# Earlier constants for a state-space layer, and a last output tile cut in 448 and 128 columns

## Chip, cores and metric

The kernel runs on one core of one Trainium2 chip. The metric is the device time of one execution in microseconds; I quote medians of several executions. A profile's own span is 1.8 us shorter than the time of the same execution.

## The reference, cut to what matters

```python
xn = layernorm(x)                                # x: 2048 x 576, bf16
# A: a diagonal state-space layer with 576 complex states
dt      = exp(log_dt)
Lam_bar = exp(dt * (Lambda_re + 1j * Lambda_im))
B_bar   = ((Lam_bar - 1) / Lam)[:, None] * (B_re + 1j * B_im)
h_t     = Lam_bar * h_(t-1) + B_bar @ xn_t       # a recurrence over 2048 steps
y_t     = 2 * real(C @ h_t) + xn_t * Dskip
# B: a gated layer
out = x + y + (sigmoid(xn @ w_gate) * (xn @ w_up)) @ w_down    # 576 -> 4608 -> 576
```

Nearly all arithmetic is in B's three products. A needs three vectors of 576 numbers (`log_dt`, `Lambda_re`, `Lambda_im`), here "the constants", from which the kernel makes two Exps and ten tables of 512 sines or cosines.

## The kernel before

TensorE (PE) does one "group" after another: 128 rows of gate and up for a block of 512 tokens, 18 matmuls, 1.94 us. ScalarE (ACT) takes a group's two halves out of PSUM (sigmoid into `sT`, copy into `uT`), VectorE (DVE) multiplies them into `hT`. PSUM holds four such pairs in turn, so group n + 4 needs the pair of group n. The first slot of the program has 24 groups; then eight output tiles `pd` take the products `hT` in.

Smaller work is queued in a list with costs. After every group the list is given some credit and emits what it can pay for, so the place of an instruction on its engine is fixed when the kernel is built:

```python
class GateUp:
    def evac(self):
        ...
        nc.scalar.activation(sT[:], self.ps[:, 0, :], ACT.Sigmoid)
        nc.scalar.copy(uT[:], self.ps[:, 1, :])
        h = hpool.tile([P, TB], BF16, name="hT", bufs=2 * FC)
        nc.vector.tensor_mul(h[:], sT[:], uT[:])
        ...
        bg.step(...)                 # emits queued work behind this group

def exp_first():
    nc.scalar.activation(dt[:], ldt[:], ACT.Exp)
    nc.vector.tensor_mul(r5[:], dt[:], lre[:])
    nc.scalar.activation(r5[:], r5[:], ACT.Exp)

# ... the queue of the first slot, in this order
for tt in range(0, 2 * TT_B):
    bg.add(1.25, lambda tt=tt: ln_resid(tt))     # 8 residual sums on VectorE
bg.gap()
bg.add(1.0, exp_first, ready=lambda: consts_at[0] is not None and consts_at[0] + 4 <= bg.now)
bg.gap()
bg.add(1.5, angles_small)
for pt in range(NU):                             # NU = 5
    for which in range(2):
        bg.add(1.35, lambda pt=pt, which=which: angle(pt, which))   # 10 angle tables on VectorE
```

`load_consts` is called among the loads of the second half of the first slot. The last output tile is computed in two halves of 288 columns, so that the first half is added and stored beside the second half's matmuls.

Of the kernel before, what the change touches and what calls it, by code (L numbers as in the profile page):

```python
# [66 lines left out]
def kernel(  # L67
# [17 lines left out]
    nc = tc.nc  # L85
    P = 128
# [3 lines left out]
    S, D = x.shape  # L90
# [15 lines left out]
    DH = D // 2  # L106
# [21 lines left out]
    def ps_pair(name):  # L128
        return psum.tile([P, 2, TB], FP32, name=name, tag="ps")
# [57 lines left out]
    lre = consts.tile([P, NU], FP32, name="lre")  # L187
    lim = consts.tile([P, NU], FP32, name="lim")
    ldt = consts.tile([P, NU], FP32, name="ldt")
    consts_at = [None]  # L190

    def load_consts():
        for (dst, src) in ((ldt, A_log_dt), (lre, A_Lambda_re), (lim, A_Lambda_im)):
            nc.gpsimd.dma_start(dst[:, 0:PT], src[0:R0].rearrange("(a p) -> p a", p=P))
            for h0 in (0, H):
                nc.gpsimd.dma_start(dst[h0:h0 + H, PT:NU], src[R0:NS].rearrange("(a b) -> a b", b=1))
        consts_at[0] = bg.now

    iota = ssmp.tile([P, TB], FP32, name="iota", tag="buim", bufs=2)
    nc.gpsimd.iota(iota[:], pattern=[[1, TB]], base=0, channel_multiplier=0,  # L200
                   allow_small_or_imprecise_dtypes=True)
# [79 lines left out]
    def split_bt():  # L281
# [8 lines left out]
    bt_loads = [  # L290
        lambda: nc.sync.dma_start_transpose(ctre[:], A_B_re[:, 0:R0]),
        lambda: nc.sync.dma_start_transpose(ctp[:], A_B_re[:, WN:D]),
        lambda: nc.sync.dma_start_transpose(ctim[:], A_B_im[:, 0:R0]),
        lambda: nc.sync.dma_start_transpose(ctw[:], A_B_im[:, WN:D]),
    ]
# [184 lines left out]
    bg = Background()  # L480
# [69 lines left out]
    def halves(ap):  # L550
        return ap.rearrange("p (a b) -> p a b", a=2)
# [10 lines left out]
    def d_step(tt, terms, final, last=False):  # L562
        acc = accs[tt]
        n = len(terms)
        pd = None if last else ps_pair("pd")

        def mm(out, i, a):
            lhsT, rhs = terms[i]
            nc.tensor.matmul(out, lhsT, rhs[:, a * DH:(a + 1) * DH], start=i == 0, stop=i == n - 1)  # L569

        if last:
            ob = lnp.tile([P, D], BF16, name="ob", bufs=2)
            for a, eng in ((0, nc.sync), (1, nc.scalar)):
                cs = slice(a * DH, (a + 1) * DH)
                pd = ps_pair("pd")
                for i in range(n):
                    mm(pd[:, 0, 0:DH], i, a)
                nc.vector.tensor_add(ob[:, cs], acc[:, cs], pd[:, 0, 0:DH])
                eng.dma_start(o[tt * P:(tt + 1) * P, cs], ob[:, cs])
            return  # L580
        for i in range(n):
            for a in range(2):
                mm(pd[:, a, 0:DH], i, a)
        if final:
            ob = lnp.tile([P, D], BF16, name="ob", bufs=2)
            nc.vector.tensor_add(halves(ob[:]), halves(acc[:]), pd[:, :, 0:DH])  # L586
            nc.sync.dma_start(o[tt * P:(tt + 1) * P, :], ob[:])
        else:
            nc.vector.tensor_add(halves(acc[:]), halves(acc[:]), pd[:, :, 0:DH])  # L589
        bg.step(n * T_DTERM - 0.76 - 0.2)  # L590


    def queue_ln(nb, part):

        tts = list(range(nb * TT_B, (nb + 1) * TT_B))

        def add(cost, fn, ready=None):
            bg.add(cost, fn, ready, urgent=True)

        if part == 0:  # L600
            for tt in tts:
                add(0.0, lambda tt=tt: load_x(tt, nc.sync))
            bg.gap(True)
            bg.gap(True)
            for tt in tts:
                add(1.05, lambda tt=tt: ln_stats(tt))
            bg.gap(True)
            add(0.0, lambda: ln_std(nb, 0, TT_B))
            bg.gap(True)
            add(0.2, lambda: ln_recip(nb, 0, TT_B))  # L610
        if part == 1:
            for tt in tts:
                add(0.9, lambda tt=tt: ln_norm(tt))
                add(0.0, lambda tt=tt: ln_dma_transpose(tt))
            add(0.0, lambda: ln_done.add(nb))
        if part == 2:
            for tt in tts:
                add(1.25, lambda tt=tt: ln_resid(tt), ready=lambda tt=tt: acc_free[0] > tt - 2 * TT_B)
                if nb == 2:
                    add(0.9, lambda tt=tt: ln_norm(tt + TT_B))  # L620
                    add(0.0, lambda tt=tt: ln_dma_transpose(tt + TT_B))
            if nb == 2:
                add(0.0, lambda: ln_done.add(3))
# [9 lines left out]
    def want_bu(i):  # L633
        if i < len(chain):
            bu_wanted.append(chain[i])

    def queue_ssm(i):
        nb, pt = chain[i]

        def bu_ready():  # L640
            return (nb, pt) in bu and bu_at[(nb, pt)] + 2 <= bg.now

        def h_ready():
            return nb < 2 or (nb - 2) in c_done

        bg.add(1.85, lambda: ssm_w(nb, pt, 0), ready=bu_ready)
        if pt < PT:
            bg.add(1.85, lambda: ssm_w(nb, pt, 1))
        else:
            bg.add(0.0, lambda: None)  # L650
        bg.add(0.0, lambda: want_bu(i + 2))
        bg.add(1.3, lambda: ssm_scan(nb, pt, 0))
        bg.add(2.0 if pt < PT else 1.2, lambda: ssm_scan(nb, pt, 1))
        bg.add(1.3, lambda: ssm_h(nb, pt, 0), ready=h_ready)
        if pt < PT:
            bg.add(1.3, lambda: ssm_h(nb, pt, 1))
        if pt == NU - 1:
            bg.add(0.0, lambda: ssm_done.add(nb))
# [55 lines left out]
    side_loads = deque()  # L714
# [68 lines left out]
    for tt in range(0, 2 * TT_B):  # L783
        bg.add(1.25, lambda tt=tt: ln_resid(tt))
    bg.gap()
    bg.add(1.0, exp_first, ready=lambda: consts_at[0] is not None and consts_at[0] + 4 <= bg.now)
    bg.gap()
    bg.add(1.5, angles_small)
    for pt in range(NU):
# [12 lines left out]
    for sb in range(NSB):  # L802
        b0 = sb * NB_SB
        for c in range(NC):
            slot = sb * NC + c
            if slot == 0:
                order = [(f, 0) for f in range(2, 10)] + [(f, 1) for f in range(0, 10)]
                order += [(f, nb) for nb in range(2) for f in range(10, 12)]
            else:
                order = [(f, b0 + nbl) for fq in range(0, FC, 4) for nbl in range(NB_SB) for f in range(fq, fq + 4)]  # L810
            if slot == 1:
                side_loads.extend(ct_loads)
                bg.add(0.0, lambda: want_bu(0))
                bg.add(0.0, lambda: want_bu(1))
                for i in range(len(chain)):
                    queue_ssm(i)
            if slot == 2:
                queue_ln(2, 0)
                queue_ln(2, 1)
            if slot == 0:  # L820
                run_groups([GateUp(slot, f, nb) for (f, nb) in order[:8]])
                catch_up_ln(1)
                order = order[8:]
                side_loads.extend([load_consts] + bt_loads)
            run_groups([GateUp(slot, f, nb) for (f, nb) in order])
            if slot == 0:
                split_bt()
                bg.add(0.0, sines)
                bg.gap()
                bg.add(2.9, per_state_q)  # L830
                for pt in range(NU):
                    bg.add(1.2, lambda pt=pt: tables(pt, 0))
                    bg.add(2.1, lambda pt=pt: tables(pt, 1))
            if slot == 2:
                catch_up(0)
                catch_up_ln(2)
                queue_ln(3, 0)
                queue_ln(2, 2)
                queue_ln(3, 2)
            for tt in range(NB_SB * TT_B):  # L840
                nbl, tl = divmod(tt, TT_B)
                nb = b0 + nbl
                final = c == NC - 1 and (nb != 1 or 1 in ssm_done)
                if final:
                    catch_up(nb)
                terms = [(hT[(f, nb)][:, tl * P:(tl + 1) * P], wd_t[(slot, f // FP)][:, f % FP, :]) for f in range(FC)]
                if final:
                    terms += c_terms(nb, tl)
                d_step(sb * NB_SB * TT_B + tt, terms, final, last=slot == n_slots - 1 and tt == NB_SB * TT_B - 1)
                if slot == 2 and final:  # L850
                    acc_free[0] = tt + 1
                if slot == 2 and tt == TT_B - 1:
                    c_done.add(0)
                if slot == 2 and tt == NB_SB * TT_B - 1:
                    glu_done[0] = True
                    if final:
                        c_done.add(1)
                between_steps()
# [30 lines left out]
```

## Time and profile before

| | before |
|---|---|
| median of 3 runs (lowest, highest) | 508.96 us (508.66, 509.38) |
| span of the profiled run | 506.5 us |
| PE busy | 500.9 us, 99% |
| VectorE, ScalarE, GpSimd busy | 64%, 40%, 19% |
| granted TensorE clock | 1.00 |

A busy share of 99% for PE says that what the other engines do can matter only where it makes PE wait. Those waits have a list of their own: who waited for whom, total, times, longest. The prediction below shows it, and the timelines around the one wait in reach; a line of a timeline is start, duration, engine, line of the kernel, operation, output and inputs, and in brackets how long the engine had been idle and what ended that.

### The profile page before, as it was taken

The page shows a single profiled execution, that of the slowest core. Times are in us where ns is not written, and L with a number is a line of the kernel's source. Part 1 is how long each engine was busy: PE and PEld are TensorE (multiplying, and loading weights), DVE is VectorE, ACT ScalarE, POOL GpSimd, SP SyncE. Part 2 cuts the span into 40 slices and gives each one's busy share as a digit, 9 for nine tenths or more (in the row PEclk, how much of TensorE's full clock was granted, in tenths as well). Part 3 has the DMA queues.
Part 4 walks back from the last instruction along what each step waited for, and adds up shares of the span by engine and source line. Part 5 has one row for each costly group of instructions (what it writes and reads, how often), then busy time and mean ns, then how long its engine had stood idle before and what let it go on. Part 6 is the DMA issues. An engine that isn't in the chain of part 4 may idle for free.

```text
span 506.5 us, 10662 instructions
## 1 busy us (share of the span) xinstructions
PE 500.9 (99%) x4536; PEld 290.1 (57%) x4536; DVE 324.1 (64%) x703; ACT 204.9 (40%) x368; POOL 96.9 (19%) x143
## 2 busy tenths in 40 slices
PE   8999999999999999999999999999999999999997
PEld 6444575444477444477754444774444774446775
DVE  6964999886888797868878767786765222221111
ACT  4767623556500756520035655006555005553000
POOL 7138420123100043110001231000431001300000
PEclk9999999999999999999999999999999999999999
DMA  8999895246220099261430652200753201600001
GB/s 211 206 181 163 204 188 98 55 110 141 49 48 25 1 145 199 58 149 37 89 77 11 155 132 55 49 25 1 160 114 79 48 25 39 171 1 4 33 25 36
DMA packets 42959, 45.59 MB, mean 90 GB/s; under 512 B 30496, under 2 KB 34336, under 8 KB 42912
## 3 DMA queue, kind: packets, MB, share of 16 engines
q0 software_dynamic: 12672, 34.23, 31.1%
q1 hardware_dynamic: 29808, 10.33, 10.7%
q8 instruction: 35, 0.57, 0.5%
q10 hardware_dynamic: 432, 0.37, 0.2%
q14 instruction: 12, 0.10, 0.1%
HBM read 34.36 MB, written 2.36 MB: 72 GB/s over the span
## 4 chain that ended last, share of the span: by engine, by line
PE 94%; DVE 3%; ACT 1%; DMA 1%; issue 0%
PE pgu L495 52%; PE pd L569 34%; PE pbu L524 7%; DVE sctab L325 1%; DVE rnd L324 1%; DMA xt<-in_A_x_dram 1%; DVE ang L349 1%; PE ptr L741 0%; DVE hT L504 0%; ACT xT L744 0%; DVE bnst L224 0%; ACT L328 0%; ACT uT L502 0%; ACT L501 0%; ACT sT L501 0%
## 5 line engine op out<-in xcount | busy, mean ns | idle before, releaser
L495 PE MATMUL pgu<-xT,wgu 64*128 64x512 bf16 (+1 forms) x2628 | 283.7, 373 | 0.0
L495 PEld LDWEIGHTS <-wgu 64*128 64x128 bf16 x2628 | 127.6, 94 | 151.1 <-issue 0.5
L569 PE MATMUL pd<-wd,hT 128*128 128x288 bf16 x1152 | 144.8, 286 | 0.4 <-DVE hT L504 0.4
L501 ACT ACTIVATE sT<-pgu 128x512 bf16<-128x512 f32 x144 | 86.4, 600 | 120.4 <-PE pgu L495 110.3
L569 PEld LDWEIGHTS <-hT 128*128 128x128 bf16 x1152 | 112.1, 98 | 31.3 <-DVE hT L504 1.5
L504 DVE TENSOR_TENSOR hT<-sT,uT 128x512 bf16<-128x512 bf16 x144 | 60.7, 423 | 100.3 <-ACT uT L502 100.1
L502 ACT CAST uT<-pgu 128x512 bf16<-128x512 f32 x144 | 83.9, 583 | 0.0
L154 POOL DMA_DIRECT2D wgu<-in_B_w_gate_dram x36 | 27.9, 776 | 227.2 <-PE pgu L495 208.2
L160 POOL DMA_DIRECT2D wd<-in_B_w_down_dram x36 | 26.6, 755 | 100.2 <-PE pd L569 100.2
L530 ACT COPY bure<-pbu 128x512 f32<-128x512 f32 x16 | 9.4, 588 | 87.8 <-PE pbu L524 75.4
L589 DVE TENSOR_TENSOR acc<-acc,pd 128x576 f32<-128x576 f32 x32 | 24.1, 752 | 24.5 <-PE pd L569 24.5
L586 DVE TENSOR_TENSOR ob<-acc,pd 128x576 bf16<-128x576 f32 x15 | 11.3, 754 | 38.0 <-PE pd L569 38.0
L524 PE MATMUL pbu<-xT,bt 64*128 64x512 bf16 x288 | 33.7, 376 | 0.0
L569 PEld LDWEIGHTS <-hst 128*128 128x128 bf16 x288 | 28.2, 98 | 7.1
L154 POOL DMA_DIRECT2D wgu<-in_B_w_up_dram x36 | 26.8, 745 | 2.7 <-DMA wgu<-in_B_w_up_dram 1.9
L569 PE MATMUL pd<-ctre,hst 128*128 128x288 bf16 x128 | 26.5, 286 | 0.0
L569 PE MATMUL pd<-ctim,hst 128*128 128x288 bf16 x128 | 26.5, 286 | 0.0
L439 DVE TENSOR_TENSOR_SCAN gre<-r,g0re,wrim 128x512 bf16<-128x512 f32 x20 | 25.6, 1279 | 0.0
L524 PEld LDWEIGHTS <-bt 64*128 64x128 bf16 x288 | 13.7, 94 | 17.1 <-issue 0.7
L446 DVE TENSOR_TENSOR_SCAN gim<-r,g0im,wrim 128x512 bf16<-128x512 f32 x16 | 20.4, 1275 | 0.0
L224 DVE BATCH_NORM_STATS2 bnst<-xt 128x6 f32<-128x288 bf16 x32 | 12.6, 435 | 2.2 <-DMA xt<-in_A_x_dram 2.2
L501 ACT ACT_TABLE_LOAD x6 | 7.7, 1283 | 15.5 <-PE pgu L495 15.4
(113 smaller groups left out, 280.8 us busy)
## 6 DMA issues: line engine op xcount, KB each, us to landing
wgu<-in_B_w_gate_dram POOLq DMA_DIRECT2D x36, 288.0 KB, 4.4
wgu<-in_B_w_up_dram POOLq DMA_DIRECT2D x36, 288.0 KB, 5.2
wd<-in_B_w_down_dram POOLq DMA_DIRECT2D x36, 288.0 KB, 6.1
out_dram<-ob SPq DMA_DIRECT2D x15, 144.0 KB, 1.8
xt<-in_A_x_dram SPq DMA_DIRECT2D x10, 144.0 KB, 2.8
xt<-in_A_x_dram POOLq DMA_DIRECT2D x4, 144.0 KB, 6.6
bt<-ctre POOLq DMA_DIRECT2D x2, 288.0 KB, 7.2
bt<-ctim POOLq DMA_DIRECT2D x2, 288.0 KB, 8.0
```

Of the source, the lines that this page charges most:

```text
L154: eng.dma_start(w[rows, :, :], src[:, fs].rearrange("(c p) f -> p c f", p=H))
L160: nc.gpsimd.dma_start(wd[:], B_w_down[f0:f0 + FP * P, :].rearrange("(n p) d -> p n d", p=P))
L224: nc.vector.bn_stats(st[:, gi, :], xt[:, gi * DH:(gi + 1) * DH])
L439: nc.vector.tensor_tensor_scan(gre[:], r_bc, w[:, 0, :], g0re[:, col], ALU.mult, ALU.add)
L446: nc.vector.tensor_tensor_scan(gim[:], r_bc, w[:, 1, :], g0im[:, col], ALU.mult, ALU.add)
L495: nc.tensor.matmul(self.ps[:, gi, cols], w[rows, c, fs], xT[self.nb][rows, c, cols], start=c == 0, stop=c == NH - 1)
L501: nc.scalar.activation(sT[:], self.ps[:, 0, :], ACT.Sigmoid)
L502: nc.scalar.copy(uT[:], self.ps[:, 1, :])
L504: nc.vector.tensor_mul(h[:], sT[:], uT[:])
L524: nc.tensor.matmul(out, w, xT[self.nb][rows, c, ts_], start=c == 0, stop=c == NH - 1)
L569: nc.tensor.matmul(out, lhsT, rhs[:, a * DH:(a + 1) * DH], start=i == 0, stop=i == n - 1)
L589: nc.vector.tensor_add(halves(acc[:]), halves(acc[:]), pd[:, :, 0:DH])
```

## The change

Its intent: load the constants early, so that the Exps need not wait for them, the angle tables end sooner and PE finds its products ready; and make the last addition and the last store small.

```diff
-    consts_at = [None]
     def load_consts():
         ...                          # nine transfers on the GpSimd queue
-        consts_at[0] = bg.now
-
+
+    load_consts()                    # right behind the fifth weight pair
     iota = ...
@@ the last output tile
-            for a, eng in ((0, nc.sync), (1, nc.scalar)):
-                cs = slice(a * DH, (a + 1) * DH)
-                pd = ps_pair("pd")
+            for eng, cs in ((nc.sync, slice(0, D - P)), (nc.scalar, slice(D - P, D))):
+                pd = ps_pair("pd")[:, 0, 0:cs.stop - cs.start]
                 ...                  # same matmuls, addition and store, on cs
@@
-    bg.add(1.0, exp_first, ready=lambda: consts_at[0] is not None and consts_at[0] + 4 <= bg.now)
+    bg.add(1.0, exp_first)
@@
-                side_loads.extend([load_consts] + bt_loads)
+                side_loads.extend(bt_loads)
```

More of the change, by code (lines that the diff above doesn't have):

```diff
@@ L572, in d_step @@
             ob = lnp.tile([P, D], BF16, name="ob", bufs=2)
-            for a, eng in ((0, nc.sync), (1, nc.scalar)):
-                cs = slice(a * DH, (a + 1) * DH)
-                pd = ps_pair("pd")
+            for eng, cs in ((nc.sync, slice(0, D - P)), (nc.scalar, slice(D - P, D))):
+                pd = ps_pair("pd")[:, 0, 0:cs.stop - cs.start]
                 for i in range(n):
-                    mm(pd[:, 0, 0:DH], i, a)
-                nc.vector.tensor_add(ob[:, cs], acc[:, cs], pd[:, 0, 0:DH])
+                    lhsT, rhs = terms[i]
+                    nc.tensor.matmul(pd, lhsT, rhs[:, cs], start=i == 0, stop=i == n - 1)
+                nc.vector.tensor_add(ob[:, cs], acc[:, cs], pd)
                 eng.dma_start(o[tt * P:(tt + 1) * P, cs], ob[:, cs])
```

## The prediction

> **What bounds the kernel now.** I read the page first: how full is TensorE, and where could it be idle?
>
> ```profile
> span 506.5 us, 10662 instructions
> PE 500.9 (99%) x4536; PEld 290.1 (57%) x4536; DVE 324.1 (64%) x703; ACT 204.9 (40%) x368; POOL 96.9 (19%) x143
> ```
>
> PE is busy for 99% of the span, at a granted clock of 1.00 in every slice. A change to loads or to the other engines can win only where PE waits, or after its last matmul. Next the list of PE's waits:
>
> ```profile
> PE pgu L733 <- DVE warm L182: 1.3, 1, 1.3
> PE pd L569 <- DVE hT L504: 0.4, 1, 0.4
> PE ptr L741 <- DVE xn L249: 0.3, 1, 0.3
> ```
>
> Two of the three lie in the start, before anything that the change touches. The third, 0.4 us, is the only one in reach. The timeline of PE shows where it is:
>
> ```profile
> 10.69 45.86 PE L495 MATMUL pgu<-xT,wgu 64*128 64x256 bf16 x450
> 56.48 2.87 PE L569 MATMUL pd<-wd,hT 128*128 128x288 bf16 x22
> 59.70 2.50 PE L569 MATMUL pd<-wd,hT 128*128 128x288 bf16 x19 [0.35 <-DVE hT L504]
> ```
>
> It is the first output tile after the first 24 gate/up groups. VectorE was still behind with the ten sine-angle tables and gave group 22's product hT late. A 288-column matmul starts every 0.1229 us (the 170 after the wait take 21.00 us in the chain, with the end of the last modelled), so the 23rd was due at 56.48 + 22 x 0.1229 = 59.18 and came at 59.70: the wait is worth **0.52 us**, a little more than the list says, because matmul ends are modelled.
>
> The angles are late because they follow the two Exps, and these were held back until the constants had been issued (35.0 to 40.5 on GpSimd) and four more groups had passed. The timeline of ScalarE around its Exps, with the groups that matter later:
>
> ```profile
> 27.82 0.58 ACT L502 CAST uT<-pgu 128x512 bf16<-128x512 f32 x1
> 28.82 0.60 ACT L501 ACTIVATE sT<-pgu 128x512 bf16<-128x512 f32 x1 [0.42 <-DVE hT L504]
> ...
> 33.28 0.60 ACT L501 ACTIVATE sT<-pgu 128x512 bf16<-128x512 f32 x1 [0.39 <-PE pgu L495]
> ...
> 42.14 1.28 ACT L328 ACT_TABLE_LOAD   x1
> 43.44 0.21 ACT L328 ACTIVATE dt<-ldt 128x5 f32<-128x5 f32 x1
> 43.88 0.21 ACT L330 ACTIVATE r<-r 128x5 f32<-128x5 f32 x1 [0.23 <-DVE r L329]
> 44.10 1.28 ACT L501 ACT_TABLE_LOAD   x1
> 45.40 0.60 ACT L501 ACTIVATE sT<-pgu 128x512 bf16<-128x512 f32 x1
> ```
>
> Counting the sigmoids from the start, the first line ends group 8, the second is group 9, the third group 12, the last group 17. The reader is to see two things. The detour costs ScalarE 3.3 us (42.14 to 45.40). And before 33 us ScalarE waits for VectorE's products; only from group 12 on is it waiting for PE, that is, up to date. VectorE at that time works off the residual sums:
>
> ```profile
> 30.63 0.76 DVE L267 TENSOR_TENSOR acc<-xt,tmpxd 128x576 f32<-128x576 bf16 x1
> 31.30 1.09 DVE L504 TENSOR_TENSOR hT<-sT,uT 128x512 bf16<-128x512 bf16 x3
> ```
>
> The first of these three hT is group 8's. VectorE had three products queued when it ended the residuals.
>
> The end, from the timeline:
>
> ```profile
> 502.79 0.46 DVE L578 TENSOR_TENSOR ob<-acc,pd 128x288 bf16<-128x288 f32 x1 [2.12 <-PE pd L569]
> 503.28 0.35 ACTq L579 DMA_DIRECT2D out_dram<-ob  x1
> ```
>
> After the last matmul: 0.46 us of addition, an issue at 503.28 that lands 1.6 us later, and 1.6 us to the span's end.
>
> **What the Trainium skill says.** "ScalarE: Activation LUTs", section "What ACT_TABLE_LOAD costs", measures 1283 ns for a load, whatever the set, and 2.66 us with the drain. The trace has the same 1.28 us, but the next instruction starts 0.02 us after it and I see no further drain; I use the trace. "DMA: Bandwidth & Descriptors", section "Issuing engines are not separate DMA queues", says that transfers from all issuers run on the same 16 engines and interleave. The trace agrees: from 18 to 21 us packets of the software queue and of the transposes move side by side, and the first two transposes land after 5.8 and 5.2 us, the last two, alone, after 3.8 and 3.9. "TensorE: Matmul & The Clock Gate", section "Back-to-back issue gap", gives N/2.4 + 2.5 ns for an isolated gap (122.5 at 288 columns; measured 122.9) but about 81 ns for a stream of weight loads and 128-column matmuls, where the formula gives 56. The 20 warming matmuls of 128 columns here, each with its weight load, take 1.29 us with 0.219 for one, so (1.29 - 0.219)/19 = 56 ns. The trace decides for 56.
>
> **The change, part one: the constants.** Their nine transfers (5.7 us of GpSimd issue before) move from 35 us to right behind the fifth weight pair, at 13.85. Each must also wait for the transfer eight before it: the issues from 6.9 us on show such waits, and the fifth pair lands only near 21 to 22 us. So I expect the issues to end near 23, all constants to have landed by 26 to 27, and the index ramp (0.58) to follow on GpSimd. It is first wanted after 36.
>
> The condition on the Exps goes as well. The instruction order of the changed kernel, which is fixed at build, puts both Exps behind the evacuation of **group 8**, not 16; on VectorE r5 = dt x lre stands after group 8's hT. Now step by step:
> 1. ScalarE ends group 8 at 28.40. Table load to 29.70, Exp of dt to 29.92.
> 2. The second Exp needs VectorE's product. VectorE is in order and has the residuals first: hT of group 8 starts at 31.30, r5 0.33 later at 31.64, done at 31.81. ScalarE idles almost 2 us.
> 3. Second Exp at 31.84; table load from 32.06 (0.22 later, as before) to 33.34; sigmoid of group 9 at 33.36 instead of 28.82; its copy starts 0.49 later and ends at 34.43.
> 4. PE has four PSUM pairs in turn, so group 13 needs group 9's pair. Group 12's last pair of matmuls starts at 33.26 - 0.376 = 32.88 and pairs follow at 1.942/9 = 0.216 us, so group 13 is due at 33.10. It can start at 34.45: a **new PE wait of 1.35 us** where none was.
> 5. Groups 10, 11, 12 are then evacuated 0.96 us apart, up to 37.3, while PE gains only one group in 1.94: groups 14 to 16 don't wait. The angles begin at about 36.2 rather than 48.2, one (1.6 us) and one hT (0.33) in each 1.94 us group, and end near 55.5. Group 22's hT is then on time, and the old wait at 59.18 is gone: -0.52.
>
> The bulk of the later work is the same with state inputs one to four groups earlier; PE never waited there, and I put 0 for it. The next weight pairs are issued up to 3 us earlier; also nothing, since no group waited for weights.
>
> **Part two: the last tile.** PE: before 2 x 21 x 0.1229 = 5.16 us; after 21 x 0.189 + 21 x 0.056 = 5.15. Nothing. The last addition: 576 columns take 0.754 us, 288 take 0.455, so 1.04 ns a column, and 128 take 0.455 - 160 x 0.00104 = 0.29: **-0.17**. The 448-column addition (0.62) lies beside the last 1.18 us of PE, and its transfer is issued before the last one. The last transfer: 144 KB land in 1.7 us, 72 KB in 1.6, so 32 KB in about 1.55: -0.05.
>
> Sum: 1.35 - 0.52 - 0.22 = **+0.61 us**; 508.96 + 0.61 = 509.6 us.
>
> **The rivals.**
> 1. *Only the intended effect.* The Exps find ScalarE with room, no new PE wait: -0.74, 508.2 us. For it: the same 3.3 us detour at 42 us cost PE nothing. Against: there ScalarE was up to date (group 16 taken as soon as PE ended), and VectorE idle; at 28 us neither holds, and step 2 adds the 2 us.
> 2. *The constants get in the way of the transposes.* Block 1's four transposes start at 17.6 and the last lands at 27.5; group 11 needs them at 33.10 - 2 x 1.942 = 29.2: 1.7 us spare. The constants are some 1,750 packets of two-byte elements that kept the engines busy for about 3.9 engine-set microseconds at 37 to 41. Wholly in front, they would make group 11 up to 2.2 us late. But a late group 11 also makes group 13 due later, so the two waits are not added: PE loses the larger, at most about 2.2 instead of 1.35: up to 510.5. Against it: part of these packets pass before the transposes fill the queue.
> 3. *The 128-column part is bound by weight loads* (81 ns instead of 56): +0.5, 510.1. The warming matmuls speak against it.
>
> **Range and chances.** About 55% for the sum as worked out (509.3 to 510.0), 20% for a smaller wait or none (508.1 to 509.2), 25% for a larger one. The three runs of before spread over 0.7 us. So 509.6, with 508.3 to 510.7. 2% is 10.2 us, far above any term here: within 2% 0.985, faster 0.005, slower 0.01.
>
> **What would show it.** Right: in PE's list of waits a wait of gate/up matmuls for ScalarE's copy of about 1 to 1.4 us at 33 us, and no wait of pd for hT; ScalarE's second Exp at about 31.8 with nearly 2 us idle before it for r; angles from about 36; a last addition of 0.29 us. Wrong: PE without a wait before 60 us (rival 1), PE waiting at group 11 for a transpose (rival 2), 128-column matmuls 80 ns apart (rival 3), or new waits on state inputs.

## The result

| | before | changed |
|---|---|---|
| median of 6 runs each (lowest, highest) | 509.11 us (508.66, 509.53) | 510.59 us (510.06, 510.95) |
| ratio | | 1.0028, 95% interval 1.0015 to 1.0041 |
| span of the profiled run | 506.5 us | 508.9 us |
| granted clock | 1.00 | 1.00 |

A ratio here is the mean time of one kernel's runs over that of the other's of the same rounds, so it is not quite the ratio of the two medians. Executions over 1.5% slower than the fastest of the same kernel are left out of the means. The change costs 1.5 us of 509: within 2%, slower, and clear of noise.

The list of PE's waits in the changed kernel:

```profile
PE pgu L494 <- ACT uT L501: 1.6, 1, 1.6
PE pgu L732 <- DVE warm L182: 1.2, 1, 1.2
PE ptr L740 <- DVE xn L248: 0.6, 1, 0.6
PE pgu L494 <- DMA xT<-xn: 0.5, 1, 0.5
```

The wait of `pd` for `hT` is gone, as intended. Two have come: the first and the last line. Where they are, in the timeline of PE:

```profile
30.26 4.06 PE L494 MATMUL pgu<-xT,wgu 64*128 64x512 bf16 x36 [0.53 <-DMA xT<-xn]
35.90 23.49 PE L494 MATMUL pgu<-xT,wgu 64*128 64x512 bf16 x216 [1.58 <-ACT uT L501]
59.32 2.87 PE L568 MATMUL pd<-wd,hT 128*128 128x288 bf16 x22
```

The first line is groups 11 and 12 (36 matmuls), which start late because block 1's transposed input has not landed. The second is group 13, which waits for a copy on ScalarE: that is the pair of group 9. The third, the first output tile, has no wait: this view ends at its 22nd matmul, and in a longer one it runs on without a break (47 matmuls up to 65 us). ScalarE in that stretch:

```profile
29.84 1.28 ACT L327 ACT_TABLE_LOAD   x1
31.14 0.21 ACT L327 ACTIVATE dt<-ldt 128x5 f32<-128x5 f32 x1
33.25 0.21 ACT L329 ACTIVATE r<-r 128x5 f32<-128x5 f32 x1 [1.91 <-DVE r L328]
33.48 1.28 ACT L500 ACT_TABLE_LOAD   x1
34.77 0.60 ACT L500 ACTIVATE sT<-pgu 128x512 bf16<-128x512 f32 x1
```

The Exps take ScalarE 4.9 us (29.84 to 34.77) and not 3.3, because it stands idle 1.91 us until VectorE has made `r5`. VectorE:

```profile
32.05 0.76 DVE L266 TENSOR_TENSOR acc<-xt,tmpxd 128x576 f32<-128x576 bf16 x1
32.73 0.42 DVE L503 TENSOR_TENSOR hT<-sT,uT 128x512 bf16<-128x512 bf16 x1
33.06 0.16 DVE L328 TENSOR_TENSOR r<-dt,lre 128x5 f32<-128x5 f32 x1
```

The last of the eight residual sums, then group 8's product, then at once `r5`, whose input `dt` had been ready since 31.35: the backlog of the residuals is what ScalarE waits for. And the end of the kernel:

```profile
505.10 0.29 DVE L577 TENSOR_TENSOR ob<-acc,pd 128x128 bf16<-128x128 f32 x1 [0.55 <-PE pd L576]
505.42 0.35 ACTq L578 DMA_DIRECT2D out_dram<-ob  x1
```

The last addition has shrunk from 0.46 to 0.29 us, but the span ends 508.9 - 505.42 = 3.5 us after the last issue, and before it was 506.5 - 503.28 = 3.2.

### The profile page after: what moved, and what is told of

Its sections match the earlier page's. It is cut to its first block, busy times and chain, and to the rows that moved or that the text cites. A ratio compares the mean times of both kernels' runs of the same rounds, so it can differ in the third digit from the quotient of the medians.

```text
span 508.9 us, 10661 instructions
## 1 busy us (share of the span) xinstructions
PE 501.1 (98%) x4536; PEld 291.4 (57%) x4536; DVE 324.1 (64%) x703; ACT 205.0 (40%) x368; POOL 96.7 (19%) x143
## 3 DMA queue, kind: packets, MB, share of 16 engines
q0 software_dynamic: 12672, 34.23, 31.4%
## 4 chain that ended last, share of the span: by engine, by line
PE 92%; DMA 3%; DVE 2%; POOL 1%; issue 0%; ACT 0%; POOLq 0%; DVEq 0%; ACTq 0%
PE pgu L494 50%; PE pd L568 34%; PE pbu L523 7%; DMA dskip_rows<-in_A_Dskip_dram 2%; DMA wgu<-in_B_w_up_dram 2%; DVE acc L266 1%; PE pd L576 1%; DVE tmpxd L263 1%; POOL wgu L154 1%; DVE hT L503 0%; ACT L500 0%; ACT uT L501 0%; POOL ident masks.py:199 0%; DVE ob L577 0%; POOL ident masks.py:197 0%
## 5 line engine op out<-in xcount | busy, mean ns | idle before, releaser
L494 PEld LDWEIGHTS <-wgu 64*128 64x128 bf16 x2628 | 129.6, 94 | 151.7 <-issue 3.4
L568 PE MATMUL pd<-wd,hT 128*128 128x288 bf16 x1128 | 141.4, 286 | 0.0
L568 PEld LDWEIGHTS <-hT 128*128 128x128 bf16 x1128 | 109.9, 98 | 30.1 <-issue 1.3
L568 PEld LDWEIGHTS <-hst 128*128 128x128 bf16 x270 | 26.4, 98 | 6.7
L568 PE MATMUL pd<-ctre,hst 128*128 128x288 bf16 x120 | 24.5, 286 | 0.0
L568 PE MATMUL pd<-ctim,hst 128*128 128x288 bf16 x120 | 24.5, 286 | 0.0
L424 DVE TENSOR_TENSOR wrim<-T,bure 128x512 bf16<-128x512 bf16 x20 | 13.7, 684 | 0.0
```

The costliest lines, as they stand in the source:

```text
L424: nc.vector.tensor_mul(w, t1, a[:])
L494: nc.tensor.matmul(self.ps[:, gi, cols], w[rows, c, fs], xT[self.nb][rows, c, cols], start=c == 0, stop=c == NH - 1)
L568: nc.tensor.matmul(out, lhsT, rhs[:, a * DH:(a + 1) * DH], start=i == 0, stop=i == n - 1)
```

## The experiments

Every run was correct. "Before" in each table is the kernel before on the same chip in the same rounds. The theory under test, A: PE waits because the Exps now sit in the stretch in which ScalarE and VectorE are behind. The rival, B: the constants' transfers get in the way of other loads, and this alone makes the loss.

### The two parts alone, and the Exps put back

`e1` leaves the last tile as before; `e2` changes only the last tile; `e3` is the changed kernel with the Exps held back to where they stood.

```diff
# e3_exps_after_16, against the changed kernel
-    bg.add(1.0, exp_first)
+    bg.add(1.0, exp_first, ready=lambda: bg.now >= 19)     # behind group 16
```

> Part one of the change alone: constants behind the fifth weight pair and the Exps behind group 8, the last tile in two halves of 288 as before. Theory A (the Exps sit in ScalarE's busiest stretch and make PE wait for group 9's pair): about 510.6 to 510.8 us, PE's waits show gate/up waiting 1.3 to 1.7 us for ScalarE's copy near 34 us and none of pd for hT. Rival B (the constants' packets delay the loads and transposes, and this alone makes the loss): the same time, but the wait that PE shows is for the transposes. Either way nearly the whole of the change's +1.5 us should be here.

> Part two alone: last tile in 448 and 128 columns, constants and Exps as before. By the prediction's sum 0.22 us less than before: 508.9 us. If the landing of the last transfer (1.9 us in the changed kernel's profile against 1.6 before) is typical, the shorter addition is given back and the time is that of before, 509.1.

> The changed kernel with one line more: the Exps wait until 16 groups are done, as in the kernel before; the constants still load early. Theory A: no PE wait for ScalarE's copy near 34 us, the wait of pd for hT (0.35 to 0.5 us) is back, a wait of up to 0.7 us for the transposes may stay: 509.0 to 509.6 us. Rival B: the loss stays, about 510.5 us.

| run | median, us | before | ratio (95%) |
|---|---|---|---|
| e1_consts_only | 510.99 | 509.01 | 1.0027 (1.0003 to 1.0051) |
| e2_tail_only | 509.35 | 509.01 | 0.9998 (0.9974 to 1.0022) |
| e3_exps_after_16 | 509.35 | 509.01 | 0.9999 (0.9973 to 1.0025) |

The loss is in part one: compared directly in the same rounds, e1 is 1.5 us slower than e2 in the mean (95% interval 0.9 to 2.1). What the last tile's cut gives, e2 cannot tell: its interval is some 1.2 us to either side, and the forecast was 0.22. And the loss goes away when only the Exps move back, with the constants still loaded early: e1 is 1.4 us slower than e3 (0.5 to 2.4). PE's waits in e3:

```profile
PE pgu L494 <- DMA xT<-xn: 1.1, 1, 1.1
...
PE pd L568 <- DVE hT L503: 0.3, 1, 0.3
```

No wait for ScalarE's copy; the wait for `hT` is back. A wait for the transposes of 1.1 us is there too, in a profiled run (510.27 us) that was among the slower ones of this kernel. So B can cost something in single executions, but A is the cause of most of the loss in the median; against the kernel before, e3's interval leaves room for up to 1.3 us that B might cost. In e1 both waits show, 1.3 for the copy and 0.5 for the transposes.

### The product on an idle engine

```diff
# e4_r5_on_gpsimd, against the changed kernel
-        nc.vector.tensor_mul(r5[:], dt[:], lre[:])
+        nc.gpsimd.tensor_mul(r5[:], dt[:], lre[:])
```

> The changed kernel with one instruction moved: the product dt x lre, 128x5, is made on GpSimd (idle then) rather than on VectorE, so the second Exp needn't wait behind VectorE's residual sums. The Exps stay behind group 8. If the wait comes from that backlog (step 2 of the prediction), ScalarE's idle 1.9 us before the second Exp shrinks to about 0.3, group 9 is evacuated some 1.5 us earlier and PE's wait for ScalarE's copy falls from 1.6 to 0.0 to 0.4 us: 508.9 to 509.5 us. If the two table loads alone are enough, the wait stays over 1 us and the time about 510.5.

Measured: 508.83 us, before 509.01; ratio 0.9994 (0.9962 to 1.0025; one execution took 511.83, which widens it). ScalarE, and PE's wait:

```profile
31.82 0.21 ACT L329 ACTIVATE r<-r 128x5 f32<-128x5 f32 x1 [0.40 <-POOL r L328]
...
33.34 0.60 ACT L500 ACTIVATE sT<-pgu 128x512 bf16<-128x512 f32 x1
```

```profile
PE pgu L494 <- ACT uT L501: 0.4, 1, 0.4
```

The table loads and both Exps still stand behind group 8, but ScalarE idles 0.40 us instead of 1.91, and PE waits 0.4 instead of 1.6. In this trace the residuals end no earlier than in the changed kernel's (the last one starts at 32.13; there at 32.05), so some 1.2 us of PE's wait are the queueing of one 0.16 us instruction behind the residuals on VectorE (1.0 us against e7 below, which has the same order of work up to the last tile, waits 1.4 us and, like e4, has no late transposes). The times agree: e4 is 1.7 us faster than e1 of the same rounds (0.3 to 3.1). This shows step 2 of the prediction.

### Where the Exps should stand

```diff
# e5_exps_after_12, against the changed kernel
+    bg.add(1.0, exp_first, ready=lambda: bg.now >= 15)     # behind group 12
# e6_consts_behind_xT: as e5; load_consts() not called at the start, but behind the transposes
+    nc.gpsimd.tensor_copy(gate, <four elements of xT[1]>)  # GpSimd waits for them
+    load_consts()
```

> The changed kernel with the Exps held until 12 groups are done: ScalarE has caught up by then, and ten angle tables still end before group 22. Theory A: neither the wait for ScalarE's copy nor the wait of pd for hT; what may stay is the wait for the transposes, which the early constants cause (0 to 1.1 us). 508.5 to 509.2 us. If the Exps' own length is what costs PE, wherever they stand among the first groups, it is still about 510.

> As the run with the Exps behind group 12, and the constants' transfers issued only when block 1's transposes have landed (GpSimd copies four elements of them first). If the constants' packets are what delays the transposes, the wait of gate/up for the transposes is gone in this profile, and no wait of PE is left after the start but the weights': 508.3 to 508.7 us, the fastest of all. If it is 508.5 to 509.2 as without this, or the wait for the transposes shows here too, the slow start of the loads causes that wait and not the constants.

| run | median, us | before | ratio (95%) |
|---|---|---|---|
| e5_exps_after_12 | 510.04 | 509.50 | 1.0005 (0.9981 to 1.0029) |
| e6_consts_behind_xT | 511.74 | 509.50 | 1.0042 (1.0017 to 1.0068) |

Both missed. In e5's profile no wait for the copy is left, as expected, but `pd` waits 0.8 us for `hT`, like the kernel before:

```profile
PE pd L568 <- DVE hT L503: 0.8, 1, 0.8
```

The profiled execution was e5's fastest (509.15 us), so what made others slower, up to 511.52, is in no trace. In e6 it is worse. Three of its six executions had a clock of 0.995 or 0.996 (512.4 to 512.86 us), but the other three, 510.94 to 511.08 at 0.999 to 1.000, are slower than the kernel before too. PE's waits, and VectorE's in the stretch from 30 to 45 us:

```profile
PE pd L567 <- DVE hT L502: 2.6, 2, 1.5
```

```profile
DVE r L327 <- DMA lre<-in_A_Lambda_re_dram: 2.5, 1, 2.5
```

I had overlooked two things. First, an angle and a product take VectorE 1.6 + 0.33 = 1.93 us, and a group takes PE 1.94. Once VectorE is behind it stays behind by the same amount, until the last angle is done. So what counts is behind which product the last angle stands, and the built order tells it: behind group 19's in the changed kernel, behind group 21's in e5. Output tile 0 wants group 22's product, so e5's tenth angle is still in its way. Second, in e6 the constants came so late (`Lambda_re` issued from 31.5 to 32.8, landing after 4.8 to 5.3 us) that VectorE waited 2.5 us for them; it made `r5` at 37.95, in e5 at 36.37, so it was 1.6 us further behind. For the wait for the transposes e6 says little: it has none, but neither has e5.

### The same kernel again, and the last store by itself

> The kernel before, unchanged, for a second trace of it: how much of what differs in the first 12 us (weights landing after 5.2 to 7.0 us in the one trace, 5.5 to 8.1 in the other) is there from run to run without any change. No wait for the transposes is expected, and a wait of pd for hT of 0.3 to 0.9 us.

The second trace of the kernel before (509.39 us, span 507.6) has its waits at the same places, with another size:

```profile
60.81 3.36 PE L569 MATMUL pd<-wd,hT 128*128 128x288 bf16 x26 [0.83 <-DVE hT L504]
```

0.83 us by the list, where the first trace had 0.35. Its last residual sum starts at 31.69, where the first trace had 30.63, because the skip row landed later (issued at 12.8, 8.6 us to landing; before 11.8 and 8.5). In the changed kernel's trace it starts at 32.05. So 1.06 of these 1.42 us of delay are there without any change.

```diff
# e7_tail_spaced, against the changed kernel: between the two parts of the last tile
+    ...                          # `spare`: one more PSUM pair
+    for _ in range(16):
+        nc.tensor.matmul(spare, terms[0][0], terms[0][1][:, 0:DH], start=True, stop=True)   # unused
```

> The changed kernel with 16 idle matmuls of 288 columns (2 us, result unused) between the two parts of the last tile, so that the first part's transfer has landed before the last one is issued. The time goes up by 2 us on purpose; what counts is the landing of the last transfer, 1.8 to 2.0 us in the four profiles with 128 columns and 1.6 in those with 288. If it overlaps with the transfer before it and this is the reason, it lands in 1.6 us here; if its 256-byte rows are the reason, 1.8 to 2.0 again.

The three answers on the last store (output and input, queue, size, us from issue to landing), of the kernel before, the changed kernel and e7:

```profile
out_dram<-ob ACTq DMA_DIRECT2D x1, 72.0 KB, 1.6
```

```profile
out_dram<-ob ACTq DMA_DIRECT2D x1, 32.0 KB, 1.9
```

```profile
out_dram<-ob ACTq DMA_DIRECT2D x1, 32.0 KB, 1.5
```

In the changed kernel the first part's store is issued at 504.58, only 0.84 us before the last one, and its packets still move at 505.5 to 506.0. With 2 us between the parts the same small store lands in 1.5 us, in this one trace. So it is the neighbour and not the 256-byte rows. How the neighbour does it is not shown: the two stores' packets do not move side by side. The last store's begin 0.86 us after its issue in e7 and 0.87 in the changed kernel, at 506.29, when the other's have ended; they end within 0.4 us in both. What grew is the time from the last packet to the landing, 0.4 us in e7 and 0.6 in the changed kernel. From the end of the last matmul to the end of the span it is 3.50 us in e7, 3.74 in both traces of the kernel before, and 3.50 to 4.07, 3.79 in the mean, in the seven traces with 448 and 128 columns at normal spacing (the changed kernel and e2 to e6, e8). The span's end varies for other reasons too: e6 ends 3.50 us after its last matmul although its store landed in 1.8.

### A version that keeps the gain

Three runs with the Exps behind group 10: late enough for ScalarE and VectorE to have come through most of the backlog, early enough for the last angle to stand behind group 19. Two of them cut the last tile at 384 columns, so that its second part takes 1.7 us and the first store is out of the way.

```diff
# e8_exps_after_10, against the changed kernel
-    bg.add(1.0, exp_first)
+    bg.add(1.0, exp_first, ready=lambda: bg.now >= 13)
# e9_after_10_tail_384: and
-    for eng, cs in ((nc.sync, slice(0, D - P)), (nc.scalar, slice(D - P, D))):
+    for eng, cs in ((nc.sync, slice(0, 384)), (nc.scalar, slice(384, D))):
# e10_gpsimd_after_10: e9, and r5 on GpSimd as in e4
```

> The changed kernel with one line more: the Exps wait until 10 groups are done. In the order of VectorE's instructions the last angle then stands behind group 19's product, as in the changed kernel, and not behind group 21's, as with the Exps behind 12. Theory: the Exps' wait for r5 is short (the residuals end near 32 to 33, dt near 33 to 34), the PE wait for ScalarE's copy is gone or under 0.4 us, and no wait of pd for hT; a wait for the transposes of up to 1 us may show. 508.3 to 508.9 us where the kernel before has 509.0 to 509.5. If it is no faster than the kernel before, the early constants' other costs eat what the angles' earlier end gives.

> As the run before this, with the last tile in parts of 384 and 192 columns instead of 448 and 128: the second part takes 21 x 0.083 = 1.7 us on PE instead of 1.2, so the first transfer is issued about 0.6 us earlier against the last one. By the spaced tail the last transfer should then land in 1.5 to 1.6 us, and the span end 3.55 to 3.65 us after the last matmul (3.74 with halves, 3.74 to 4.07 with 448 and 128 at normal spacing). Under 0.2 us in the time: 508.2 to 508.8.

> As the last, with r5 = dt x lre on GpSimd. With the Exps behind group 10 VectorE has nearly ended its residuals, so this should make no more than 0.3 us of difference, in runs where the load of the skip row is late: 508.1 to 508.8 us.

| run | median, us | before | ratio (95%) |
|---|---|---|---|
| e8_exps_after_10 | 509.29 | 509.34 | 1.0001 (0.9989 to 1.0014) |
| e9_after_10_tail_384 | 508.83 | 509.34 | 0.9986 (0.9973 to 0.9998) |
| e10_gpsimd_after_10 | 508.98 | 509.34 | 0.9988 (0.9974 to 1.0002) |

All of PE's waits in e9:

```profile
PE pgu L732 <- DVE warm L182: 1.3, 1, 1.3
PE ptr L740 <- DVE xn L248: 0.6, 1, 0.6
PE pgu L494 <- DMA wgu<-in_B_w_up_dram: 0.4, 1, 0.4
```

All three lie in the first 10 us, before the parts that were changed: neither the copy nor `hT` is waited for. The second Exp waited 0.23 us for `r5`, and the last store landed in 1.5 us. e8 is no faster than the kernel before. Its profiled run was its slowest (510.24 us), and in it group 11 started at 31.49 with 1.73 us of waiting, while the last transpose was issued at 26.5 and landed 4.9 us later, at 31.4. The list names a sigmoid for this wait, but that had long been done. So e8 missed what was expected of it, and e9 and e10 came out just above their ranges. The 0.46 us between e8 and e9 are more than the cut of the last tile explains (in traces some 0.3 us at the end: 3.79 against 3.52, 3.69 and 3.29 in e9, e10 and e11); the rest is within the spread of five runs. Which part of e9 makes it faster than the kernel before, by 0.7 us (0.1 to 1.4), was not taken apart further.

### Is it the constants that delay the transposes?

PE waited for the transposes in the changed kernel, e1, e3, e8 and e10, not in e4, e5, e7 and e9, and in none of the four traces without early constants (two of before, e2, e6). The four transposes' issues spanned 7.3 to 8.5 us in those four, 7.5 to 10.7 in the nine others. That looks like a cause, so I doubled it:

```diff
# e11_consts_twice, against e9
-        for (dst, src) in ((ldt, A_log_dt), (lre, A_Lambda_re), (lim, A_Lambda_im)):
+        for (dst, src) in ((ldt, A_log_dt), (spare[0], A_log_dt), (lre, A_Lambda_re), (spare[1], A_Lambda_re),
+                           (lim, A_Lambda_im), (spare[2], A_Lambda_im)):
```

> The fastest version so far (Exps behind group 10, last tile 384 and 192) with every transfer of the constants issued twice, the second copy into tiles that nobody reads: some 1,750 more packets of two-byte elements on the software queue while block 1's transposes run. If the constants' packets are what delays the transposes, the four transposes' issues span over 10 us (7.3 to 8.5 us in the four traces without early constants, 7.5 to 10.7 in the nine with), PE waits 1 to 3 us for them at group 11, and the time is 509.5 to 511.5 us. If the waits for the transposes are only the run-to-run variation of the loads, the span stays within 7.5 to 10 us and the time near 508.8.

Measured: 508.60 us, before 509.40, ratio 0.9981 (0.9967 to 0.9994). The issues spanned 7.7 us and PE waited 0.8 us at group 11. Twice the packets do not make the time longer: between 22 and 28 us the transposes' queue moved 3,681 packets beside 1,990 small ones of the software queue, and in the first trace of before, where the software queue was empty then, 4,687. So the queue moved less beside the small packets, but doubling them did not delay the end of the transposes beyond what other runs show.

The spans of the issues hide something that the packets show. In all 13 traces without doubled constants the last transpose lands 6.4 to 7.8 us after the last packet of the first five weight pairs, with early constants or without. In the five of them in which PE waited, those weights had ended at 22.8 to 23.7; in the others at 21.1 to 22.3, or at 23.0 in e4, where PE's first groups were 0.5 us later than in the changed kernel's trace. In e11 they ended at 21.8, and the last transpose landed 8.7 us later, at 30.5. So the wait goes with the end of the weights' loads, and the doubled constants seem to have cost the transposes about 1 us, though the time did not show it. Whether early constants make the weights end later (waits in six of ten traces with them, in none of four without) stays **open**, and so does what else does; the loads of the first 13 us, which differ from run to run in every kernel, are a candidate that no run here isolates. This run is also a second measurement of e9's order of work, and again faster than the kernel before.

## Why the prediction was right, and where its sizes were off

It said 509.6 us with 508.3 to 510.7; measured were 510.59. Expected was a rise of 0.6 us, and it was 1.5. That this lies inside the range, by 0.1 us, is in part luck: four sizes were wrong, and one of them made up for half a microsecond of the others. One of its signs of being wrong came too, PE waiting at group 11 for a transpose, beside its signs of being right, which came some 1.4 us later than it had named.

- **The old wait goes, a new one comes**: right, at the engine, the group and the cause that it named. The durations of steps 1 to 3 held to 0.1 us (table load 1.28, idle 1.91 where it said almost 2, sigmoid of group 9 0.22 + 1.30 us after the second Exp), and e4 shows the cause.
- **Step 4, the size of the new wait**: 1.35 us predicted, from the due start of group 13 to its start. Reckoned in the same way it was 1.76 in the changed kernel, 1.48 in e1 and 1.56 in e7 (by the list, which counts from modelled ends, 1.58, 1.30 and 1.42). Right in kind, and too small by 0.1 to 0.4 us.
- **Step 2's clock time** was off by 1.4 us: group 8's product starts at 32.73 and not 31.30. I had taken one trace of the kernel before as the time of the residuals; its second trace ends them 1.06 us later. The prediction took a quantity for fixed that depends on how fast the loads are in an execution.
- **"The two waits are not added", in rival 2**, is the step that failed. It supposed that the transposes might be late while group 9's evacuation kept its time. In the changed kernel's trace both are late: group 11 is due at 11.06 + 18.53 = 29.59 (18.53 is what it took from the same matmul before) and starts at 30.26, which is 0.67 us; group 13 is due at 30.26 + 3.88 = 34.14 and starts at 35.90, another 1.76. Against the times that the prediction used, group 11 came 1.04 us late and the residuals, and with them `r5`, 1.42, so the second wait did not shrink but grew by about the difference.
- **The wait removed** was mis-sized: 0.52 from one trace. In the second trace of before the 23rd matmul was due at 57.11 + 22 x 0.1229 = 59.81 and came at 60.81: 1.00 us.
- **The end**: -0.17 for the addition, and PE's 5.15 us, were right (parts of 0.189 and 0.056 us a matmul; rival 3 is out). The landing term failed: -0.05 predicted, +0.3 measured. I had scaled it with size and not seen that the two stores come within 0.84 us; e7 shows that. So -0.22 became about 0: the stretch from the last matmul to the end is 3.79 us in the mean of seven traces, where it was 3.74. The times of e2 are too coarse to tell 0 from -0.22.
- **The constants' issues** ended at 24.98 and not near 23, and the last landed 4.6 us after its issue, near 29 and not 27. Nothing waited for it.

With the second trace of before, which is near the median, the account closes (it is one pair of traces, and the pair was chosen afterwards): +0.67 and +1.76 for the two waits and -1.00 for the old one are +1.43; the stretch up to the first output tile had 0.24 us more in that trace of before than in the first (46.03 against 45.79), -0.24; the end +0.09. Sum +1.28, and the spans differ by 508.9 - 507.6 = 1.3.

## What to carry to other kernels

Removing a wait's cause early is worth what the engine can take at that time: the Exps were ready sooner, but sooner meant behind eight residual sums in VectorE's fixed order, with two table loads around them and PSUM only four groups deep. Ask of every moved instruction what stands before it on its own engine and on the engine that it waits for, and how many groups of slack the buffers leave. When work comes at the rate of the bottleneck (here 1.93 us against 1.94), a lag never shrinks, and the place of the last piece in the order decides; and read such places from more than one trace.

## What the Trainium skill lacked or had wrong

- "TensorE: Matmul & The Clock Gate", section "Back-to-back issue gap": it gives about 81 ns a matmul for a sustained stream of weight loads and 128-column matmuls. The last part of the changed kernel is such a stream, with a new weight each time: its first matmul starts at 503.73 and its 21st at 504.85, so 1.12/20 = 56 ns, which is what the page calls the isolated gap.
- "ScalarE: Activation LUTs", section "What ACT_TABLE_LOAD costs": 1.28 us for the load agrees in every trace here; the further drain of 1.38 us does not show: the Exp starts 31.14 - 29.84 = 1.30 us after the load's start. What the page lacks is the case that cost the time here: two switches around two tiny Exps, with a product of another engine between them, held ScalarE for 3.3 us at best and 4.9 at worst.
- "DMA: Bandwidth & Descriptors", section "Anatomy of one DMA — SWDGE (gpsimd) path", tells a fixed cost of some 2.0 us for a transfer from GpSimd. These stores go from other queues, and no page that I used tells how a small store fares right behind another: 32 KB landed in 1.8 to 2.0 us when issued 0.84 us behind a 112 KB store from another queue, and in 1.5 with 2.8 us between the issues.
- "SBUF — State Buffer", section "Who interferes with whom", says that VectorE in a two-port mode and GpSimd lock each other out. The changed kernel's trace may show this: the fp32 rounding step of an angle took 0.43 us, but 0.63 to 0.70 in the three angles between 45.9 and 50.9 us, when GpSimd issued transfers one after another. Two such steps beside other issues, at 40.12 and 43.96, took 0.43 too, and no run tests whether the lock is the reason. The page gives no size for VectorE's loss while GpSimd issues transfers; if this is one, it was 0.2 to 0.3 us a step.
